# Linear attention beside a gated MLP on one core: a new prologue, tiles turned by DMA, and the up units in one phase

## The chip, the cores and the metric

The kernel runs on one core of one Trainium2 chip. The core has a matrix engine (TensorE, PE in the profile; its weight loads are listed as PEld), a vector engine (VectorE, DVE), an activation engine (ScalarE, ACT), a general engine (GpSimd, POOL) and a queue engine (SyncE, SP), which here only issues transfers. The engines run side by side, each through its own list of instructions in order, and wait for each other on semaphores. Sixteen DMA engines move data. The metric is the device time of one execution in microseconds, smaller is better; shown is the median of the runs.

## The reference

The input x has 2048 tokens of width 512, the attention 32 heads of width 16, the MLP an inner width of 1792. Everything is bfloat16.

```python
xn = _layernorm(x, axis=-1)
return x + _A_ref(xn, A_wqkv, A_w_phi, A_wo) + _B_ref(xn, B_w_gate, B_w_up, B_w_down)

# _A_ref: attention with a softmax feature map
pq = jnp.einsum("bhsd,hdf->bhsf", q, w_phi)
pk = jnp.einsum("bhsd,hdf->bhsf", k, w_phi)
phi_q = jnp.concatenate([_softmax(pq, axis=-1), _softmax(-pq, axis=-1)], axis=-1)
phi_k = jnp.concatenate([_softmax(pk, axis=-1), _softmax(-pk, axis=-1)], axis=-1)
kv = jnp.einsum("bhsf,bhsd->bhfd", phi_k, v)
z  = jnp.einsum("bhsf->bhf", phi_k)
num = jnp.einsum("bhqf,bhfd->bhqd", phi_q, kv)
den = jnp.einsum("bhqf,bhf->bhq", phi_q, z)[..., None] + 1e-6
o = num / den          # then @ wo

# _B_ref: gated MLP without an activation
h = g * u              # g = xn @ w_gate, u = xn @ w_up; then h @ w_down
```

The sums over all tokens in `kv` and `z` split the work into two phases: no query result can be formed before the last key has been added.

## The kernel before

The 2048 tokens are 16 tiles of 128. Every tensor lies in one SBUF arena, and PSUM has eight banks of 512 columns, named by their number.

**Normalization and turning.** `ln_stats` (bn_stats and bn_aggr on DVE, L324 and L325, then Ln and Exp on ACT through the helper at L186) gives mean and inverse deviation, `ln_apply` (DVE, L333) normalizes a tile into one of four `xn` slots, and `x_transpose` turns it: four transposes on PE (L343) into a bank, and a copy by ACT into `xnT`. All matmuls on x read `xnT`.

**Weights.** `w_fold` (L307) multiplies the turned query or key weights by the block-diagonal feature weights, four small matmuls into a bank and a copy by ACT. Folding is done four times for the keys (`w_fold(1, dt)`) and four times for the queries.

**Key and value phase.** For each tile `features("ek", t, 1)` makes the key features: four matmuls of 512 columns (L205, the helper of all the wide matmuls), two exponentials on ACT, a reduce on DVE (L365), a reciprocal (L369) and a ratio (L373), and a product on POOL (L375). `v_stage` makes the values and scales them on DVE (L388; a small copy on POOL at L387). `kv_acc` adds the tile into banks 0 and 1 (L400, eight matmuls of 68 columns). `kv_finish` masks the sums.

**Query phase.** `features("eq", t, 0)` and `q_transpose` (a transposing DMA, L427) make a turned query tile; `num_stage` (L441) multiplies it by the sums into banks 0 and 1, DVE forms the quotient (L449, L452, L453), and another transposing DMA (L457) turns the result. `out_tile` adds 14 matmuls of the MLP's second half and four of the attention's output in one bank; DVE adds x (L490), and the tile is stored (L492).

**Up units.** An `up_unit` is the MLP's first half for 128 inner columns and 512 tokens: eight wide matmuls into a pair of banks, (4, 5) or (6, 7) in turn, a copy of the gate by ACT and a product on DVE (L475). There are 56. The key and value phase has two in each iteration, and the rest stand between the query phase's stages.

**Order.** The steps are recorded in program order, and a planner (`_order`) then forms each engine's list. On PE the program order is kept. On the other engines, and on SP's queue, the planner takes the step that is ready first by its own costs: so many nanoseconds for a step, 200 from one engine to another, and for transfers one stream of 360 bytes a nanosecond in the order of their issue, with 550 for an issue and 1700 for a landing. A step placed on a list waits there on semaphores for what it needs, and everything behind it on that engine waits with it.

Of the kernel before, what the change touches and what calls it, by code (L numbers as in the profile page):

```python
# [16 lines left out]
FF = 1792  # L17
# [4 lines left out]
FSL = 256  # L22
# [4 lines left out]
class _Step:  # L27
    __slots__ = ("eng", "fn", "idx", "deps", "sig", "lane", "semval", "known", "waits", "is_out", "cost", "seq",
                 "finish")

    def __init__(self, eng, fn, idx, lane, cost):
        self.eng = eng
        self.fn = fn
        self.idx = idx
        self.deps = []
        self.sig = False
        self.lane = lane
        self.semval = None
        self.known = {}
        self.waits = []  # L40
        self.is_out = False
        self.cost = cost
        self.seq = 0
        self.finish = 0.0


class _Sched:


    def __init__(self):  # L50
        self.steps = []
        self.writer = {}
        self.readers = {}
        self.dma_count = 0

    def _record(self, st, reads, writes, free=()):
        deps = {}

        def need(d, raw):
            if d is None or d is st:  # L60
                return
            if d.lane == st.lane and (st.eng == PE or not raw):
                return
            deps[id(d)] = d

        for k in reads:
            need(self.writer.get(k), True)
            self.readers.setdefault(k, []).append(st)
        for k in writes:
            w = self.writer.get(k)  # L70
            assert w is None or w is st or self.readers.get(k) or k in reads or st.lane == w.lane or k in free, f"{k} is overwritten unread"
            need(w, False)
            for r in self.readers.get(k, ()):
                need(r, False)
            self.writer[k] = st
            self.readers[k] = []
        st.deps = list(deps.values())

    def step(self, eng, fn, reads, writes, cost):
        st = _Step(eng, fn, len(self.steps), eng, cost)  # L80
        self.steps.append(st)
        self._record(st, reads, writes)
        return st

    def dma(self, eng, fn, reads, writes, nbytes, is_out=False, free=()):
        st = _Step(eng, fn, len(self.steps), ("dma", self.dma_count), nbytes / 360.0)
        self.dma_count += 1
        st.sig = True
        st.is_out = is_out
        self.steps.append(st)  # L90
        self._record(st, reads, writes, free)
        return st
# [18 lines left out]
def _build(nc, es, A_x, A_wqkv, A_w_phi, A_wo, B_w_gate, B_w_up, B_w_down, out):  # L111
# [11 lines left out]
    RK, RQ, RP = 3, 3, 8  # L123
# [17 lines left out]
    alloc("ostg", 3 * 512)  # L141
    alloc("wphi", NQ * 16)
# [8 lines left out]
    alloc("lnv", 2 * NT)  # L151
    alloc("sums", 2 * 16 * 64)
# [60 lines left out]
    mask = sb("mask", 0, CW)  # L213
    eps_f = sbf("eps", 0, 1)
# [28 lines left out]
    def load_gu(eng, s):  # L243
        sl = slice(s * FSL, (s + 1) * FSL)
        load_w(eng, wg_v[:, :, sl], B_w_gate[:, sl].rearrange("(q p) f -> p q f", p=128), ("wg", s), 262144)
        load_w(eng, wu_v[:, :, sl], B_w_up[:, sl].rearrange("(q p) f -> p q f", p=128), ("wu", s), 262144)

    load_w(ACT, wphi_v, bass.AP(tensor=A_w_phi.tensor, offset=A_w_phi.offset, ap=[[16, 128], [2048, NQ], [1, 16]]),
           "wphi", 16384)
    load_x(0, 2)  # L250
    load_qkT(1)
    load_x(2, 2)
    load_w(SP, wv_v, A_wqkv[:, 1024:1536].rearrange("(q p) j -> p q j", p=128), "wv", 524288)
    load_gu(SP, 0)
# [4 lines left out]
    load_qkT(0)  # L259
    load_gu(SP, 3)  # L260
    load_x(12, 4)
    for s in range(4, FF // FSL):
        load_gu(SP, s)
    load_w(SP, wd_v, B_w_down.rearrange("(f p) j -> p f j", p=128), "wd", 1835008)
    load_w(SP, wo_v, A_wo.rearrange("(q p) j -> p q j", p=128), "wo", 524288)


# [33 lines left out]
    def w_fold(w, dt):  # L301
        b = misc_bank()

        def fn(e):
            ins = None
            for jt in range(NQ):
                ins = e.matmul(bank(b, jt * 128, 128), lhsT=wT_v[:, w, jt, dt * 128:(dt + 1) * 128],  # L307
                               rhs=wbd_v[:, jt, :], start=True, stop=True)
            return ins
        sc.step(PE, fn, [("wT", w)] + [("wbd", jt) for jt in range(NQ)], [("ps", b)], 4 * 60.0)  # L310
        act(Wp_v[:, w, dt, :], bank(b), [("ps", b)], [("Wp", w, dt)])
# [5 lines left out]
    rstd = sbf("rstd", 0, NT)  # L317

# [13 lines left out]
    def ln_apply(t):  # L332
        dve(lambda e: e.tensor_scalar(out=xn_tile(t), in0=x_tile(t), scalar1=mv_v[:, t, 0:1], scalar2=rstd[:, t:t + 1],  # L333
                                      op0=ALU.subtract, op1=ALU.mult),
            [("x", t), ("mv", t), ("rstd", t)], [("xn", t % 4)], 512, 0.27)
# [18 lines left out]
    def features(name, t, w):  # L354
        s = t % RK
        e_v = sb(name, s * 1024, 1024).rearrange("p (h k f) -> p h k f", h=H, k=2)
        b = misc_bank() if w else 2
# [24 lines left out]
    def v_stage(t):  # L382
        s = t % RK
        b = misc_bank()
        mm(bank(b), [(xnT(q, t * 128, 128), wv_v[:, q, :]) for q in range(NQ)], [("xnT", t), "wv"], b)
# [49 lines left out]
    def num_stage(t):  # L435
        ph = ph_tile(t)

        def fn(e):
            ins = None
            for c in range(8):  # L440
                ins = e.matmul(bank(c // 4, (c % 4) * CW, CW), lhsT=ph[:, c, :], rhs=kvz_v[:, c, :], start=True,  # L441
                               stop=True)
            return ins
        sc.step(PE, fn, [("phT", t % RP), ("kvz", 0), ("kvz", 1)], [("ps", 0), ("ps", 1)], 8 * 31.0)
        nd = psum[:, 0:1024].rearrange("p (b r) -> p b r", b=2)[:, :, 0:4 * CW].rearrange(
# [5 lines left out]
            [("sums", t % 8), ("ps", 0), ("ps", 1)], [("den", r)], 32)  # L451
# [4 lines left out]
            [("w", r), ("ps", 0), ("ps", 1)], [("o", t % 3)], 512)  # L456
# [6 lines left out]
    def up_unit(ft, sg, pairs):  # L463
# [4 lines left out]
        sl = ft * 128 // FSL  # L468
# [7 lines left out]
            [("ps", bu), ("g", s)], [("hT", ft, sg)], 512)  # L476

    outs = [0]

    def out_tile(t):  # L480
        i = outs[0]
        outs[0] += 1
        b = 3 if ups else 4 + i % 4
        sg = t // 4
        tok = slice(t * 128, (t + 1) * 128)
        mm(bank(b), [(hT_v[:, ft, tok], wd_v[:, ft, :]) for ft in range(NF)],
           [("hT", ft, sg) for ft in range(NF)] + ["wd"], b, stop=False)
        mm(bank(b), [(oT_tile(t)[:, q, :], wo_v[:, q, :]) for q in range(NQ)], [("phT", t % RP), "wo"], b, start=False)
        stg = sb("ostg", (i % 3) * 512, 512)
        dve(lambda e: e.tensor_tensor(out=stg, in0=bank(b), in1=x_tile(t), op=ALU.add),  # L490
            [("ps", b), ("x", t)], [("ostg", i % 3)], 512)
        sc.dma(SP, lambda e: e.dma_start(out_flat[tok, :], stg), [("ostg", i % 3)], [("out", t)], 131072, is_out=True)  # L492
# [3 lines left out]

    def next_up(pairs):
        if ups:
            ft, sg = ups.pop(0)
            up_unit(ft, sg, pairs)  # L500

    PAIRS = [(4, 5), (6, 7)]

    def up(n=1):
        for _ in range(n):
            if ups:
                up_unit(*ups.pop(0), PAIRS)

    ln_stats(0, 1)
    ln_apply(0)  # L510
    ln_stats(1, 1)
    ln_apply(1)
    ln_stats(2, 2)
    for t in range(2, 4):
        ln_apply(t)
    x_transpose(0)
    x_transpose(1)
    for dt in range(NQ):
        w_fold(1, dt)
    x_transpose(2)  # L520
    x_transpose(3)
    wq_steps = [lambda dt=dt: w_fold(0, dt) for dt in range(NQ)]
    for t in range(NT + 2):
        if t < NT:
            features("ek", t, 1)
        if t in (0, 2, 4):
            ln_stats(4 + 2 * t, 4)
        up()
        if 2 * t + 4 < NT:
            ln_apply(2 * t + 4)  # L530
            x_transpose(2 * t + 4)
        elif wq_steps and t >= 6:
            wq_steps.pop(0)()
        if 0 <= t - 1 < NT:
            v_stage(t - 1)
        up()
        if 2 * t + 5 < NT:
            ln_apply(2 * t + 5)
            x_transpose(2 * t + 5)
        elif wq_steps and t >= 6:  # L540
            wq_steps.pop(0)()
        if t >= 2:
            kv_acc(t - 2)
        if t >= NT - 1:
            features("eq", t - NT + 1, 0)
            q_transpose(t - NT + 1)
            up()
    kv_finish()
    up()
    oq = list(range(NT))  # L550
    for t in range(NT):
        if t + 3 < NT:
            features("eq", t + 3, 0)
            q_transpose(t + 3)
        up()
        num_stage(t)
        up()
        if t >= 2:
            out_tile(oq.pop(0))
    up(len(ups))  # L560
    while oq:
        out_tile(oq.pop(0))
# [10 lines left out]
def _order(sc):  # L573
# [9 lines left out]
    fixed = {PE: [st for st in steps if st.eng == PE]}  # L583
# [9 lines left out]
    while len(order) < len(steps):  # L593
        best = None
        for e, lst in ready.items():
            if e in fixed:
                lst = [p for p in lst if p[1] == fixed[e][pos[e]].idx] if pos[e] < len(fixed[e]) else []
# [9 lines left out]
        if e in fixed:  # L607
            pos[e] += 1
        st = steps[idx]
        if isinstance(st.lane, tuple):  # L610
# [98 lines left out]
```

## Time and profile before

| | us |
|---|---|
| median of three runs | 237.48 |
| lowest and highest | 235.88, 238.23 |
| the profiled execution | 238.51 |
| its span, first to last instruction | 236.8 |

| engine | busy us | share of the span |
|---|---|---|
| PE | 218.5 | 92% |
| PEld | 105.5 | 45% |
| DVE | 146.0 | 62% |
| ACT | 82.7 | 35% |
| POOL | 42.8 | 18% |

In the lines of the profile a row names the source line, the engine, the operation, what is written and read with its shape, a count, and then the busy time and the mean duration of one in nanoseconds, and the idle time before it with what ended it. A timeline or chain row begins with its start and its length in microseconds. "Releaser" is what an idle engine was waiting for last. A slice string has 40 digits, one for each fortieth of the span (5.92 us), in tenths. A windows row has the stretch and its length, the busy time and count of PE, PEld, DVE, ACT and POOL (or of PE alone), and then the clock granted to PE, with 1.00 for full, the mean busy share of the DMA engines and the GB/s moved.

### The profile page before, as it was taken

How to read it: one execution, taken by the hardware profiler on the slowest of the kernel's cores; microseconds unless marked ns; L12 is line 12 of the kernel's file. 1: busy time of each engine (PE TensorE's matmuls, PEld its weight loads, DVE VectorE, ACT ScalarE, POOL GpSimd, SP SyncE). 2: the span in 40 equal slices, each digit the busy share in tenths (PEclk: the TensorE clock that was granted, in tenths of full speed). 3: DMA queues.
4: the chain of work that ended last, by engine and by line, in shares of the span. 5: the costliest groups of instructions: out<-in, count | busy, mean ns of one | idle time of the engine just before them, and what ended most of it. 6: DMA issues, size and time to landing. Idle time of an engine off the chain costs nothing.

```text
span 236.8 us, 3283 instructions
## 1 busy us (share of the span) xinstructions
PE 218.5 (92%) x1255; PEld 105.5 (45%) x1280; DVE 146.0 (62%) x282; ACT 82.7 (35%) x157; POOL 42.8 (18%) x65
## 2 busy tenths in 40 slices
PE   0397969999999999999999999999999999999994
PEld 0243424555544444444444444444444454444441
DVE  2369995766666666666657784654564567775421
ACT  3374626555543343334344541232132132110000
POOL 6002220222222223321211211101101111111000
PEclk9999988999999999999999999999999999999999
DMA  7999990000000000000022265064125135754411
GB/s 150 324 261 281 312 312 6 1 3 0 0 3 0 0 0 3 0 0 3 0 46 44 44 93 106 27 91 89 22 66 91 32 82 116 125 114 89 69 46 44
DMA packets 44993, 18.32 MB, mean 77 GB/s; under 512 B 30897, under 2 KB 44977, under 8 KB 44977
## 3 DMA queue, kind: packets, MB, share of 16 engines
q1 hardware_dynamic: 44448, 18.09, 33.6%
q8 instruction: 10, 0.16, 0.3%
q10 hardware_dynamic: 528, 0.02, 0.1%
q14 instruction: 7, 0.05, 0.1%
HBM read 8.67 MB, written 2.10 MB: 45 GB/s over the span
## 4 chain that ended last, share of the span: by engine, by line
PE 89%; DVE 3%; DMA 2%; issue 2%; ACT 1%; SPq 1%
PE ps L205 83%; PE ps L343 2%; DMA arena<-in_A_x_dram 2%; PE ps L441 2%; PE ps L400 2%; ACT arena L186 1%; SPq L241 1%; PE ps L307 1%; DVE arena L475 1%; DVE arena L324 1%; DVE arena L365 0%; DVE arena L369 0%; DVE arena L333 0%; DVE arena L490 0%; SPq L226 0%
## 5 line engine op out<-in xcount | busy, mean ns | idle before, releaser
L205 PE MATMUL ps<-arena 128*128 128x512 bf16 x903 | 207.7, 383 | 1.4
L205 PEld LDWEIGHTS ps<-arena 128*128 128x128 bf16 x928 | 88.5, 98 | 101.9 <-issue 3.3
L186 ACT ACTIVATE arena<-ps 128x512 bf16<-128x512 f32 (+1 forms) x144 | 79.6, 597 | 124.0 <-PE ps L205 108.2
L365 DVE TENSOR_REDUCE arena<-arena 128x64 f32<-128x1024 bf16 x32 | 38.9, 1216 | 33.9 <-ACT arena L186 33.9
L375 POOL TENSOR_TENSOR arena<-arena 128x512 bf16<-128x512 bf16 x32 | 34.0, 1061 | 90.6 <-DVE arena L373 86.1
L475 DVE TENSOR_TENSOR arena<-ps,arena 128x512 bf16<-128x512 f32 x56 | 38.4, 685 | 12.8 <-PE ps L205 12.8
L490 DVE TENSOR_TENSOR arena<-ps,arena 128x512 bf16<-128x512 f32 x16 | 11.1, 691 | 30.0 <-PE ps L205 30.0
L387 POOL CAST arena<-arena 128x32 bf16<-128x32 f32 x16 | 5.2, 326 | 78.5 <-DVE arena L369 75.0
L343 PE MATMUL ps<-arena 128*128 128x128 bf16 x64 | 6.9, 242 | 13.4 <-DVE arena L333 13.1
L324 DVE BATCH_NORM_STATS2 arena<-arena 128x6 f32<-128x512 bf16 x16 | 10.3, 672 | 6.9 <-DMA arena<-in_A_x_dram 6.9
L343 PEld LDWEIGHTS ps<-arena 128*128 128x128 bf16 x64 | 5.1, 108 | 17.4 <-DVE arena L333 14.1
L453 DVE TENSOR_TENSOR arena<-ps,arena 128x512 bf16<-128x512 f32 x16 | 11.1, 691 | 0.5
L388 DVE TENSOR_TENSOR arena<-ps,arena 128x512 bf16<-128x512 f32 x16 | 10.2, 636 | 0.1
L369 DVE RECIPROCAL arena<-arena 128x64 f32<-128x64 f32 x16 | 8.7, 542 | 0.0
L333 DVE TENSOR_SCALAR arena<-arena 128x512 bf16<-128x512 bf16 x16 | 7.1, 486 | 1.6 <-ACT arena L186 1.6
L441 PEld LDWEIGHTS ps<-arena 128*128 128x128 bf16 x128 | 6.2, 97 | 3.8
L400 PEld LDWEIGHTS ps<-arena 128*128 128x128 bf16 x128 | 5.9, 97 | 2.4
L441 PE MATMUL ps<-arena 128*128 128x68 bf16 x128 | 6.7, 194 | 0.0
L400 PE MATMUL ps<-arena 128*128 128x68 bf16 x128 | 6.7, 194 | 0.0
L373 DVE TENSOR_TENSOR arena<-arena 128x32 f32<-128x32 f32 x32 | 5.9, 184 | 0.2
L452 DVE RECIPROCAL arena<-arena 128x32 f32<-128x32 f32 x16 | 5.6, 349 | 0.3
L371 DVE RECIPROCAL arena<-arena 128x32 f32<-128x32 f32 x16 | 5.5, 347 | 0.2
(17 smaller groups left out, 20.1 us busy)
## 6 DMA issues: line engine op xcount, KB each, us to landing
out_dram<-arena SPq DMA_DIRECT2D x16, 128.0 KB, 1.7
arena<-in_B_w_gate_dram SPq DMA_DIRECT2D x7, 256.0 KB, 6.0
arena<-in_B_w_up_dram SPq DMA_DIRECT2D x7, 256.0 KB, 6.0
arena<-in_B_w_down_dram SPq DMA_DIRECT2D x1, 1792.0 KB, 10.1
arena<-in_A_x_dram SPq DMA_DIRECT2D x3, 512.0 KB, 6.3
arena<-in_A_x_dram SPq DMA_DIRECT2D x2, 256.0 KB, 3.6
arena<-in_A_wqkv_dram SPq DMA_DIRECT2D x1, 512.0 KB, 5.0
arena<-in_A_wo_dram SPq DMA_DIRECT2D x1, 512.0 KB, 10.7
```

Source lines behind the costliest of these rows:

```text
L186: return sc.step(ACT, lambda e: e.activation(out=out_ap, in_=in_ap, func=func, scale=scale, **kw), reads, writes, 130.0 + 0.833 * n)
L205: ins = e.matmul(out_ap, lhsT=l, rhs=r, start=start and i == 0, stop=stop and i == npair - 1, **kw)
L324: dve(lambda e, t=t: e.bn_stats(stats_v[:, t, 0:6], x_tile(t)), [("x", t)], [("st", t)], 512)
L343: ins = e.transpose(bank16(b, q * 128, 128), xn_tile(t)[:, q * 128:(q + 1) * 128], ident)
L365: dve(lambda e: e.tensor_reduce(out=sm, in_=e_v, axis=AX.X, op=ALU.add), [(name, s, 0), (name, s, 1)], [("sums", sr)], 1024)
L375: pool(lambda e: e.tensor_tensor(out=e_v[:, :, 1, :], in0=e_v[:, :, 1, :], in1=rat[:, :, None].to_broadcast([128, H, 16]), op=ALU.mult), [ ...
L388: dve(lambda e: e.tensor_tensor(out=vs_tile(t)[:, :, 0:16], in0=bank(b).rearrange("p (h f) -> p h f", h=H), in1=rp.unsqueeze(2).to_broadca ...
L400: ins = e.matmul(bank(c // 4, (c % 4) * CW, CW), lhsT=ek[:, c * 128:(c + 1) * 128], rhs=vs[:, c * CW:(c + 1) * CW], start=(t == 0 and c % ...
L441: ins = e.matmul(bank(c // 4, (c % 4) * CW, CW), lhsT=ph[:, c, :], rhs=kvz_v[:, c, :], start=True, stop=True)
L453: dve(lambda e: e.tensor_tensor(out=o_tile(t).rearrange("p (b h f) -> p b h f", b=2, f=16), in0=nd[:, :, :, 0:16], in1=w_v[:, r].unsqueeze ...
L475: dve(lambda e: e.tensor_tensor(out=hT_v[:, ft, sg * 512:(sg + 1) * 512], in0=bank(bu), in1=g, op=ALU.mult), [("ps", bu), ("g", s)], [("hT ...
L490: dve(lambda e: e.tensor_tensor(out=stg, in0=bank(b), in1=x_tile(t), op=ALU.add), [("ps", b), ("x", t)], [("ostg", i % 3)], 512)
```

## The change

**Loads.** x comes as tile 0, tile 1, tiles 2 and 3, and then in fours. The value weights, the feature weights and the first gate and up slice are issued on ACT's queue. The slices of gate and up are now one of 256 columns and three of 512. The last slice, tiles 12 to 15, the turned query weights and the two output weights are issued on SP within iterations 1, 3 and 5 of the key and value phase.

**Pinning.** Steps recorded while `sc.pin` is set keep their order among themselves on every engine, as all PE steps do; the others may still be placed between them.

**Prologue.** DVE zeroes 512 columns (in the place of `hT`), and PE multiplies them 16 times into bank 5. Then come statistics of tiles 0 and 1, their normalization, statistics of tiles 2 and 3, the transposes of tiles 0 and 1, normalization of tiles 2 and 3, the values of tiles 0 and 1 in banks 0 and 1 (scaled later), the transposes of tiles 2 and 3, and the key folds, whose evictions alternate between ACT and DVE. One up unit follows.

**Tiles 4 to 15** are normalized by ACT (a scale and a bias, the bias by POOL) and turned by a DMA from SP instead of PE and ACT.

**Phases.** The key and value phase has three up units in most iterations; in its last iterations `features` and `q_transpose` of query tiles 0 to 5 are added. The query phase has no up units but one at its start: for each tile a `num_stage`, the `out_tile` of the tile before, and the features of the tile seven ahead. `num_stage` alternates between banks 0, 1 and 2, 3. The last output tile is made in two halves of 256 columns. The key features have four slots instead of three.

```diff
-FSL = 256
+SLICES = [(0, 256), (256, 512), (768, 512), (1280, 512)]
...
+    sc.pin = True
+    load_x(0, 1)
+    load_w(ACT, wv_v, A_wqkv[:, 1024:1536].rearrange("(q p) j -> p q j", p=128), "wv", 524288)
+    load_x(1, 1)
+    load_x(2, 2)
     load_w(ACT, wphi_v, ...
-    load_x(0, 2)
     load_qkT(1)
-    load_x(2, 2)
-    load_w(SP, wv_v, ...
-    load_gu(SP, 0)
+    load_gu(ACT, 0)
     load_x(4, 4)
     load_gu(SP, 1)
     load_gu(SP, 2)
     load_x(8, 4)
+    sc.pin = False
...
+    dve(lambda e: e.memset(zero, 0.0), [], ["zero"], 256)
...
     def ln_apply(t):
+        if t < 4:
+            dve(...)
+            return
+        nb = nbias[:, t:t + 1]
+        pool(lambda e: e.tensor_scalar(out=nb, in0=mv_v[:, t, 0:1], scalar1=rstd[:, t:t + 1], scalar2=-1.0,
+                                       op0=ALU.mult, op1=ALU.mult), [("mv", t), ("rstd", t)], [("nb", t)], 1)
+        act(xn_tile(t), x_tile(t), [("x", t), ("rstd", t), ("nb", t)], [("xn", t % 4)], func=ACTF.Identity,
+            scale=rstd[:, t:t + 1], bias=nb)
+
+    def x_turn(t):
+        o = sb("xnT", 0, NQ * S_TOK).rearrange("p (q s) -> p q s", q=NQ)[:, :, t * 128:(t + 1) * 128]
+        sc.dma(SP, lambda e: e.dma_start_transpose(o, xn_tile(t)), [("xn", t % 4)], [("xnT", t)], 131072)
...
+    sc.pin = True
+    warm(16)
     ln_stats(0, 1)
+    ln_stats(1, 1)
     ln_apply(0)
-    ln_stats(1, 1)
     ln_apply(1)
-    ln_stats(2, 2)
-    for t in range(2, 4):
-        ln_apply(t)
+    ln_stats(2, 1)
+    ln_stats(3, 1)
     x_transpose(0)
     x_transpose(1)
-    for dt in range(NQ):
-        w_fold(1, dt)
+    ln_apply(2)
+    ln_apply(3)
+    v_matmul(0, 0)
+    v_matmul(1, 1)
     x_transpose(2)
     x_transpose(3)
+    for dt in range(NQ):
+        w_fold(1, dt, (2, 3, 6, 7)[dt])
+    sc.pin = False
+    up()
...
     for t in range(NT + 2):
         if t < NT:
             features("ek", t, 1)
-        if t in (0, 2, 4):
-            ln_stats(4 + 2 * t, 4)
+        if t % 2 == 0 and 4 + t < NT:
+            ln_stats(4 + t, 2)
         up()
...
+        x_next(t + 4)
+        late_loads(t)
+        if 2 <= t - 1 < NT:
+            b = misc_bank()
+            v_matmul(t - 1, b)
+            v_scale(t - 1, b)
+        if t < 2:
+            v_scale(t, t)
+        else:
+            up()
             kv_acc(t - 2)
+            up()
+        if 7 < t < 12:
+            w_fold(0, t - 8)
+        if t >= NT - 4:
+            features("eq", t - NT + 4, 0)
+            q_transpose(t - NT + 4)
+        if t >= NT - 2:
             up()
     kv_finish()
...
+    q_next(6)
+    up(len(ups))
+    num_stage(0)
+    q_next(7)
+    for t in range(1, NT):
         num_stage(t)
+        out_tile(t - 1)
+        q_next(t + 7)
+    out_tile(NT - 1, 2)
...
-    fixed = {PE: [st for st in steps if st.eng == PE]}
+    fixed = {e: [st.idx for st in steps if st.eng == e and st.pin] for e in (PE, ACT, DVE, POOL, SP)}
...
-                lst = [p for p in lst if p[1] == fixed[e][pos[e]].idx] if pos[e] < len(fixed[e]) else []
+            if pos[e] < len(fixed[e]):
+                lst = [p for p in lst if not steps[p[1]].pin or p[1] == fixed[e][pos[e]]]
```

## What is predicted

> **What bounds the kernel now.** I read the busy shares and slices first, then the chain, then PE's timeline.
>
> ```profile
> span 236.8 us, 3283 instructions
> PE   0397969999999999999999999999999999999994
> GB/s 150 324 261 281 312 312 6 1 3 0 0 3 0 0 0 3 0 0 3 0 46 44 44 93 106 27 91 89 22 66 91 32 82 116 125 114 89 69 46 44
> PE 89%; DVE 3%; DMA 2%; issue 2%; ACT 1%; SPq 1%
> L205 PEld LDWEIGHTS ps<-arena 128*128 128x128 bf16 x928 | 88.5, 98 | 101.9 <-issue 3.3
> ...
> 14.51 1.90 PE ps L205 x4
> ...
> 22.24 0.22 PE ps L343 x4
> 22.46 2.59 PE ps L205 x12
> ...
> 131.38 0.26 PE ps L441 x8
> ...
> 233.91 0.69 DVE arena L490
> ```
>
> PE carries 89% of the chain, and its slices are full from the seventh to the last: there only less PE work helps. The chain gives full-speed prices: a wide matmul 2.59/12 = 0.216 us, a tile's four transposes 0.22, a fold (four matmuls of the same shape) as much, and eight small matmuls of `kv_acc` or `num_stage` 0.26. There are 928 wide matmuls (by their weight loads; some matmul records are missing), 16 transposed tiles, 8 folds and 32 groups of small ones: 200.3 + 3.5 + 1.8 + 8.2 = 213.8 us. The last matmul ends at 233.9, so PE loses 20.1 us, and 2.9 us follow it.
>
> ```profile
> 9.19 1.04 PE L343 MATMUL ps<-arena 128*128 128x128 bf16 x8 [9.19 <-DVE arena L333]
> 14.51 3.99 PE L205 MATMUL ps<-arena 128*128 128x512 bf16 x12
> 20.12 0.40 PE L343 MATMUL ps<-arena 128*128 128x128 bf16 x4 [1.62 <-DVE arena L333]
> ...
> 32.98 0.40 PE L343 MATMUL ps<-arena 128*128 128x128 bf16 x4 [2.30 <-DVE arena L333]
> 33.22 4.44 PE L205 MATMUL ps<-arena 128*128 128x512 bf16 x12
> ...
> 3.86 1.29 DVE L324 BATCH_NORM_STATS2 arena<-arena 128x6 f32<-128x512 bf16 x2 [3.86 <-DMA arena<-in_A_x_dram]
> 8.12 0.70 DVE L324 BATCH_NORM_STATS2 arena<-arena 128x6 f32<-128x512 bf16 x1 [2.76 <-DMA arena<-in_A_x_dram]
> 8.73 0.72 DVE L333 TENSOR_SCALAR arena<-arena 128x512 bf16<-128x512 bf16 x2
> ...
> 12.94 1.29 DVE L324 BATCH_NORM_STATS2 arena<-arena 128x6 f32<-128x512 bf16 x2 [0.29 <-DMA arena<-in_A_x_dram]
> ...
> 15.46 0.30 DVE L325 BATCH_NORM_AGGREGATE arena<-arena 128x2 f32<-128x6 f32 x2
> ```
>
> All 20 us are lost before 37.5: 9.2 before the first transposes, 3.6 in the thin prologue (1.76 us of work in 5.32), 1.4 on slow matmuls from 14.51, gaps of 1.6 and 2.3, and 1.7 on the slow dozen from 33.2. The DVE rows give the cause: DVE runs in order, and the planner had put the statistics of tile 2 ahead of tile 0's normalization. They waited for x until 8.12, so tile 0 was normalized only at 8.73, though its own statistics had begun at 3.86. The later gaps end on the same kind of wait.
>
> **The change, part by part.** PE's work first. Twelve tiles leave PE for the transposing DMA: 12 x 0.22 = 2.6 us less. The split of the last output keeps its columns, and eight matmuls of 68 columns in 0.26 us show that weight loads hide well below 256 columns: 0. That leaves 211.2 us. The dummies run before any tile is ready. Should all 16 run as slowly as the four that took 1.90 from 14.51, 0.475 each, they fill 7.6 us from about 1.3 and end at 8.9; at the full rate they end at 4.8. The first copies on ACT begin at 8.45 in any case (next), so at worst 0.5 to 1 us, and that is hidden by a later wait of 2.3: 0.
>
> ```profile
> L186 ACT ACTIVATE arena<-ps 128x512 bf16<-128x512 f32 x128 | 70.2, 597 | 110.1 <-PE ps L205 108.2 <-PE ps L307 1.7
> 5.26 0.71 ACT L186 ACTIVATE arena<-arena 128x1 f32<-128x1 f32 x4 [3.17 <-DVE arena L325]
> 0.81 0.44 SPq L226 DMA_DIRECT2D arena<-in_A_x_dram  x1
> 1.31 2.60 SPq L241 DMA_TRANSPOSE arena<-in_A_wqkv_dram  x1
> 3.97 0.56 SPq L226 DMA_DIRECT2D arena<-in_A_x_dram  x1
> ```
>
> Prologue. Tiles 2 and 3 are now issued at 1.8 instead of 3.97, ahead of the 2.6 us issue of the key weights, but beside value weights on ACT's queue. Bounds for their landing: 4.9 (3.05 us after issue, as tiles 0 and 1) and 8.1 (as now); I take 6.0, because 0.5 MB of x and 0.5 MB of values, at some 250 GB/s between the first two slices (150 and 324), need 4 us after the first 2. Their two statistics end at 7.9, and ACT, whose pinned order puts the copies of tiles 0 and 1 behind their Ln and Exp, copies at 8.45 to 9.65 (0.6 each). Then `v_matmul` 0 and 1 (1.7) to 10.8, transposes 2 and 3 to 11.3, their copies to 12.4. The first fold uses the bank of tile 3's transpose, so folds run 12.5 to 13.4, and the first up unit (8 x 0.216) to 15.1. By then PE has done 16 wide matmuls, four tiles and four folds: 3.45 + 0.88 + 0.88 = 5.2 us. So 206.0 us remain from `features(0)` on, which could begin at 15.1.
>
> It will not, I think. Pinned steps keep their order only among themselves; loose ones may slip between, by the planner's modelled landing. It models tiles 4 to 7 as landed just after `ln_apply(3)` and the folds much later, so all four statistics of 4 to 7 stand on DVE ahead of the two fold evictions now given to DVE, and their Ln and Exp on ACT ahead of the other two. Now these tiles land at 12.94. The same 2.6 MB stand ahead of them, in two queues; I take 12.5 (bounds 11.3, where the slices' sum reaches 2.6 MB, and 12.94). Four statistics took 2.8 us (12.94 to 15.76): 15.3. Ln and Exp 0.9: 16.2. Two evictions on ACT 1.2: `features(0)` at 17.4, a PE gap of 2.3 us.
>
> The Trainium skill, DMA: Bandwidth & Descriptors, section Issuing engines are not separate DMA queues, says that issuing from several engines saves only the sequencer's issue time, since the same 16 DMA engines carry all. By it the tiles would land at 12.94 as before and the sum below would be 0.4 us longer. The row agrees so far as it shows a 2.6 us issue in front of x.
>
> ```profile
> 12.90:17.50 4.60, 4.29 (x19) 1.80 (x18) 2.82 (x8) 3.01 (x7) 0.00 (x0) 1.00 1.25 266
> 17.50:33.00 15.50, 11.48 (x64) 5.40 (x65) 15.42 (x33) 7.96 (x18) 3.13 (x5) 1.00 1.07 303
> ...
> L365 DVE TENSOR_REDUCE arena<-arena 128x64 f32<-128x1024 bf16 x32 | 38.9, 1216 | 33.9 <-ACT arena L186 33.9
> L475 DVE TENSOR_TENSOR arena<-ps,arena 128x512 bf16<-128x512 f32 x56 | 38.4, 685 | 12.8 <-PE ps L205 12.8
> L369 DVE RECIPROCAL arena<-arena 128x64 f32<-128x64 f32 x16 | 8.7, 542 | 0.0
> L388 DVE TENSOR_TENSOR arena<-ps,arena 128x512 bf16<-128x512 f32 x16 | 10.2, 636 | 0.1
> L373 DVE TENSOR_TENSOR arena<-arena 128x32 f32<-128x32 f32 x32 | 5.9, 184 | 0.2
> L375 POOL TENSOR_TENSOR arena<-arena 128x512 bf16<-128x512 bf16 x32 | 34.0, 1061 | 90.6 <-DVE arena L373 86.1
> ```
>
> A second block of this kind follows. Between tiles 4 to 7 and 8 to 11 stand wider slices, 2.1 MB, and 0.5 MB of x itself: 2.62 MB at 303 GB/s is 8.6 us, a landing at about 21.1. The planner lets three of their statistics (2.2 with an aggregate) go ahead of `features(0)`'s sums: reduce ends at 24.3, the product of the second up unit at 25.0. Its banks are wanted by the fourth unit, which PE reaches at 17.4 + 3 x 0.86 + 2 x 1.73 = 23.4: 1.6 us. The next product waits for recip, reduce, ratio, value scaling (0.54 + 1.22 + 0.18 + 0.64) and ends 3.2 after: 1.5 more; the third wait is 0.1. Together 3.2 us. Bounds: 0 and 4.6 (landing as in the rivals).
>
> After that an iteration has 32 wide matmuls, 7.2 us, against 1.22 + 0.54 + 0.18 + 0.64 + 3 x 0.69 + 0.84 = 5.5 on DVE and about 3.9 on ACT, where tile 4 on are now normalized: 0. POOL's small bias step precedes that on ACT; bounded by POOL's row, 0 to 1.06 a tile, hidden by four iterations of lead. On SP each turn waits for ACT, and behind it wait the last gate slice, tiles 12 to 15, query weights and both output weights. The earliest needed, the gate slice, is used only in iteration 4, about 14 us after its turn in the queue: 0.
>
> ```profile
> L457 SPq DMA_TRANSPOSE arena<-arena x16: 1189/1196/1271, 135.2 to 223.9; - x16
> DMA to landing us min/median/max: 2.4/2.4/4.2
> ...
> SPq L457 <- DVE arena L453: 34.1, 10, 5.3
> ...
> 222.61 0.18 DVE L449 SCALAR_TENSOR_TENSOR arena<-arena,ps 128x32 f32<-128x32 f32 x1
> ...
> 223.21 0.69 DVE L453 TENSOR_TENSOR arena<-ps,arena 128x512 bf16<-128x512 f32 x1
> ```
>
> The query phase loses its up units, its cover. A tile there is 22 wide matmuls and a `num_stage`, 5.0 us. From `num_stage(t)` to its turned result: 1.3 on DVE (222.61 to 223.90) and 2.4 landing, 3.7. PE needs it behind `out_tile(t-1)`, features, `num_stage(t+1)` and 14 matmuls: 3.9 + 0.9 + 0.3 + 3.0 = 8.0. Cover holds. Only the first tile has no `out_tile` before it: 4.4 after the start of its `num_stage`, against 0.26 + 3.7 + one reduce 1.22 = 5.2: 0.8 us once (0 to 2). At the end only half of the tile is evicted last, half of 0.69: 2.9 becomes 2.6.
>
> Sum: 17.4 + 206.0 + 3.2 + 0.8 + 2.6 = 230.0 us of span. The profiled execution took 238.51 with a span of 236.8, 1.71 outside, and the median 237.48 lies 1.03 below it. So 231.7 on its terms, 230.7 for the median.
>
> **The rivals.**
> Through: tiles 4 to 11 block nobody; `features(0)` starts at 15.1: 15.1 + 206.0 + 0.8 + 2.6 = 224.5, median 225.2. For it: the prologue's own order is pinned. Against: the rows at 8.12 and 12.94 show DVE held by x.
> Half: tiles 4 to 7 block, 8 to 11 land in time: 226.8 of span. Here the clock counts.
>
> ```profile
> 34.00:34.50 0.50, 0.50 (x4) 0.60 1.02 320
> ...
> 37.50:38.00 0.50, 0.50 (x14) 0.99 0.00 0
> ```
>
> After the idle 2.30 us, granted clock fell to 0.5 from 34.2 to 37.5: half of 3.4 us, 1.7, is lost. My gap of 2.3 would do likewise: 228.5, median 229.2. In the forecast itself this loss lies under DVE's debt. TensorE: Matmul & The Clock Gate, Part 1 of the Trainium skill, gives an idle window of about 3.4 us before the clock halves; by it this rival would give 226.8. The row disagrees: 2.30 sufficed.
> Debt: tiles 4 to 7 land at 12.94, and 2.62 MB go at 266 GB/s, so 8 to 11 land at 22.8. That is 0.4 more for the start, 1.4 more of debt, and 1.7 if the clock's loss adds: 233.5, median 234.2. The change then nearly fails at its purpose.
> Slower: SP holds each turned result behind the next query turn. That one is ready 3.9 + 0.9 + 1.2 + 1.2 + 0.5 + 1.06 = 8.7 after `num_stage(t)`; with 1.25 issue and 2.4 landing, the result comes at 12.4 instead of 8.0, and eight tiles lose 4.4: 35 us, median 266. It decides from 0.85 a tile (6.8 over eight). Against: SP's waits at L457 are for that tile's own DVE result, so it stands in front.
>
> **How the numbers follow.** Forecast 0.41, half 0.17, through 0.24, debt 0.13, slower 0.05. I predict 230.7. From 224.0 to 235.0: the low end cuts the part of "through" in which tiles 2 and 3 land at 4.9 and the first output waits for nothing (223.3), the high end the rest of "debt" and "slower". A measurement tells about 1% from no change, so faster means below 235.1: three cases and 0.05 of "debt", 0.87; the rest of "debt", 0.08, is the same; slower 0.05.
>
> **What would show it.** First transposes near 6 to 8, `v_matmul` 0 near 9; `features(0)` near 17 behind ACT or DVE, with DVE's idle there ended by x; DVE without idle around 21 to 30; a saturated PE after; waits under 1 us at the first output. PE's end before 220 would refute the two blocks, PE gaps at every query tile the cover.

## The result and the profile after

| | before | changed |
|---|---|---|
| median us | 237.46 | 230.31 |
| lowest and highest | 235.88, 238.23 | 229.74, 231.65 |
| profiled execution, span | 238.51, 236.8 | 229.74, 228.0 |

The ratio is 0.9715, with a 95% interval from 0.9649 to 0.9782: the changed kernel is faster, by 7.15 us of the medians. The forecast was 230.7. The two profiled spans differ by 8.8 us, and the account below is made between them. One execution of a later run, the one without dummies, fell into a slow state (238.79 us, the five others 230.63 to 232.16) and is left out of its median below.

First the page of the changed kernel: its span, PE's slices, and the shares of the chain that ended last.

```profile
span 228.0 us, 3302 instructions
PE   7389999999999999999999999989999999999995
PE 92%; DVE 2%; DMA 2%; ACT 2%; issue 1%; SPq 0%; DVEq 0%
```

The slices are full from the fourth on instead of the seventh. The digit 7 at the start is no gain: those are the dummy matmuls. PE's timeline of the changed kernel shows the front row by row (start, length, what, and in brackets the idle time before it).

```profile
1.26 4.97 PE L536 MATMUL ps<-arena 128*128 128x512 bf16 x16 [1.26 <-DVE arena L273]
7.02 0.40 PE L365 MATMUL ps<-arena 128*128 128x128 bf16 x4 [0.79 <-DVE arena L345]
7.83 0.40 PE L365 MATMUL ps<-arena 128*128 128x128 bf16 x4 [0.42 <-DVE arena L345]
10.49 3.29 PE L212 MATMUL ps<-arena 128*128 128x512 bf16 x8 [2.26 <-ACT arena L193]
13.58 0.94 PE L365 MATMUL ps<-arena 128*128 128x128 bf16 x8
15.47 1.05 PE L314 MATMUL ps<-arena 128*128 128x128 bf16 x16 [0.96 <-ACT arena L193]
16.37 11.39 PE L212 MATMUL ps<-arena 128*128 128x512 bf16 x52
...
151.50 1.04 PE L212 MATMUL ps<-arena 128*128 128x512 bf16 x4 [1.05 <-DVE arena L500]
```

The chain of the same kernel puts the end of the folds at 16.53, and its later rows give the steady price.

```profile
1.25 4.36 DMA arena<-in_A_x_dram
...
15.47 1.05 PE ps L314 x16
16.53 11.22 PE ps L212 x52
27.75 0.26 PE ps L423 x8
28.01 6.91 PE ps L212 x32
...
157.54 0.26 PE ps L466 x8
157.79 4.75 PE ps L212 x22
...
225.51 0.42 DVE arena L517
```

Here the whole change can be read. From 16.53 to the end PE waits once, 1.05 us at 151.50. Up to 16.53 it has done 3.5 us of useful work (eight wide matmuls, four tiles, four folds at full rate), so 13.0 are lost in front, against 20.1 before. That is 7.1 of the 8.8 us. The turned tiles give 2.6 (12 x 0.22), the shorter end 0.4 (228.0 less 225.5 against 2.9), and the new wait takes 1.05. These make 9.05; small pauses take the rest. No run takes the new front back alone, or parts its loads from its pinned order, so the 7.1 us rest on the waits in the two profiles.

Three things in these rows matter later. The eight value matmuls took 3.29 us where eight take 1.73 at full rate. They waited 2.26 us for ACT. And no gap at all stands before the first features, which follow the first up unit at 18.3. The clock explains the first. These are half-microsecond windows of PE in the changed kernel (length, busy time and count of PE, granted clock, DMA share, GB/s).

```profile
2.00:2.50 0.50, 0.50 (x2) 1.00 0.82 207
...
10.50:11.00 0.50, 0.50 (x2) 0.84 1.08 336
11.00:11.50 0.50, 0.50 (x3) 0.50 1.11 352
...
13.50:14.00 0.50, 0.50 (x5) 0.50 1.05 334
14.00:14.50 0.50, 0.50 (x6) 0.75 1.14 361
```

The dummies had done what they are there for. 16 in 4.97 us is 0.31 each, between the full rate of 0.216 and half of it: they began slowly, two in the window at 2.00 against four in a window at full rate, although the granted clock reads 1.00 there. Then PE did nothing for 2.26 us, and soon after the real work began the granted clock fell to 0.50 for some 3.4 us. So PE is slow in two ways here: at a granted clock of 0.50, and in its first work, where the profile's clock shows nothing.

DVE's timeline of the changed kernel answers to the rows shown of before.

```profile
5.64 0.69 DVE L335 BATCH_NORM_STATS2 arena<-arena 128x6 f32<-128x512 bf16 x1 [1.57 <-DMA arena<-in_A_x_dram]
...
6.46 0.50 DVE L345 TENSOR_SCALAR arena<-arena 128x512 bf16<-128x512 bf16 x1
...
11.63 1.29 DVE L335 BATCH_NORM_STATS2 arena<-arena 128x6 f32<-128x512 bf16 x2 [1.16 <-DMA arena<-in_A_x_dram]
...
16.12 1.29 DVE L321 CAST arena<-ps 128x512 bf16<-128x512 f32 x2 [1.67 <-PE ps L314]
...
19.17 1.29 DVE L335 BATCH_NORM_STATS2 arena<-arena 128x6 f32<-128x512 bf16 x2 [0.18 <-DMA arena<-in_A_x_dram]
...
20.45 0.66 DVE L335 BATCH_NORM_STATS2 arena<-arena 128x6 f32<-128x512 bf16 x1
21.03 1.20 DVE L387 TENSOR_REDUCE arena<-arena 128x64 f32<-128x1024 bf16 x1
22.15 0.68 DVE L500 TENSOR_TENSOR arena<-ps,arena 128x512 bf16<-128x512 f32 x1
```

Tile 0 is normalized (L345) at 6.46 instead of 8.73. The order is the forecast one: the statistics of tiles 4 to 7 before the fold evictions (L321), and three of tiles 8 to 11 before the first reduce (L387). But here DVE waits 1.67 us for the folds themselves, so its statistics held up no eviction. What differs is how late that was: x landed at 11.6 and 19.2 instead of 12.5 and 21.1.

### The profile page after: what moved, and what is told of

Its sections match the earlier page's. It is cut to its first block, busy times and chain, and to the rows that moved or that the text cites. A ratio compares the mean times of both kernels' runs of the same rounds, so it can differ in the third digit from the quotient of the medians.

```text
span 228.0 us, 3302 instructions
## 1 busy us (share of the span) xinstructions
PE 218.7 (96%) x1266; PEld 105.7 (46%) x1266; DVE 146.9 (64%) x276; ACT 83.3 (37%) x161; POOL 45.3 (20%) x77
## 4 chain that ended last, share of the span: by engine, by line
PE 92%; DVE 2%; DMA 2%; ACT 2%; issue 1%; SPq 0%; DVEq 0%
PE ps L212 88%; DMA arena<-in_A_x_dram 2%; PE ps L423 2%; PE ps L466 2%; ACT arena L193 2%; PE ps L314 1%; DVE arena L335 1%; DVE arena L500 0%; DVE arena L336 0%; DVE arena L345 0%; DVE arena L387 0%; PE ps L365 0%; DVE arena L517 0%; SPq L234 0%; DVEq L724 0%
## 5 line engine op out<-in xcount | busy, mean ns | idle before, releaser
L212 PE MATMUL ps<-arena 128*128 128x512 bf16 (+1 forms) x946 | 208.0, 377 | 3.3 <-ACT arena L193 2.3
L212 PEld LDWEIGHTS ps<-arena 128*128 128x128 bf16 x946 | 90.3, 98 | 103.5 <-ACT arena L193 2.4
L193 ACT ACTIVATE arena<-ps 128x512 bf16<-128x512 f32 (+1 forms) x128 | 70.0, 597 | 100.0 <-PE ps L212 95.6
L387 DVE TENSOR_REDUCE arena<-arena 128x64 f32<-128x1024 bf16 x32 | 38.7, 1214 | 20.7 <-ACT arena L193 20.7
L500 DVE TENSOR_TENSOR arena<-ps,arena 128x512 bf16<-128x512 f32 x56 | 38.3, 685 | 21.3 <-PE ps L212 20.8
L517 DVE TENSOR_TENSOR arena<-ps,arena 128x512 bf16<-128x512 f32 (+1 forms) x17 | 11.2, 660 | 23.7 <-PE ps L212 23.7
L193 ACT ACTIVATE arena<-arena 128x2 f32<-128x2 f32 (+2 forms) x32 | 13.8, 460 | 9.6 <-DVE arena L336 5.8
L478 DVE TENSOR_TENSOR arena<-ps,arena 128x512 bf16<-128x512 f32 x16 | 11.1, 691 | 0.5
L411 DVE TENSOR_TENSOR arena<-ps,arena 128x512 bf16<-128x512 f32 x16 | 10.4, 649 | 0.1
L423 PEld LDWEIGHTS ps<-arena 128*128 128x128 bf16 x128 | 6.2, 97 | 3.8
L466 PEld LDWEIGHTS ps<-arena 128*128 128x128 bf16 x128 | 6.2, 97 | 3.8
L395 DVE TENSOR_TENSOR arena<-arena 128x32 f32<-128x32 f32 x32 | 6.8, 213 | 0.4
L536 PE MATMUL ps<-arena 128*128 128x512 bf16 x16 | 5.0, 480 | 1.3 <-DVE arena L273 1.3
L350 POOL TENSOR_SCALAR arena<-arena 128x1 f32<-128x1 f32 x12 | 2.9, 265 | 15.1 <-ACT arena L193 15.1
```

Of the source, the lines that this page charges most:

```text
L193: return sc.step(ACT, lambda e: e.activation(out=out_ap, in_=in_ap, func=func, scale=scale, **kw), reads, writes, 130.0 + 0.833 * n)
L212: ins = e.matmul(out_ap, lhsT=l, rhs=r, start=start and i == 0, stop=stop and i == npair - 1, **kw)
L387: dve(lambda e: e.tensor_reduce(out=sm, in_=e_v, axis=AX.X, op=ALU.add), [(name, s, 0), (name, s, 1)], [("sums", sr)], 1024)
L411: dve(lambda e: e.tensor_tensor(out=vs_tile(t)[:, :, 0:16], in0=bank(b).rearrange("p (h f) -> p h f", h=H), in1=rp.unsqueeze(2).to_broadca ...
L423: ins = e.matmul(bank(c // 4, (c % 4) * CW, CW), lhsT=ek[:, c * 128:(c + 1) * 128], rhs=vs[:, c * CW:(c + 1) * CW], start=(t == 0 and c % ...
L466: ins = e.matmul(bank(b0 + c // 4, (c % 4) * CW, CW), lhsT=ph[:, c, :], rhs=kvz_v[:, c, :], start=True, stop=True)
```

## The experiments

The theory after the profile: PE is the bound from 16.5 on, and the front is a chain through the landing of tile 1, DVE's statistics in pinned order, ACT's copies behind them, and the values at half clock. Behind that chain stand the two blocks that the prediction named, just covered. The rivals: the dummies do save something; or the blocks are not there; or the gain came from moving the up units.

All ratios are to the kernel before on the same chip. The first four runs stand beside each other, then the next four, then the last four.

| run | median us | ratio | 95% interval |
|---|---|---|---|
| changed kernel again | 231.67 | 0.9787 | 0.9752 to 0.9822 |
| no dummies | 230.71 | 0.9764 | 0.9729 to 0.9798 |
| dummies up to the first value | 231.98 | 0.9802 | 0.9774 to 0.9831 |
| turned on PE | 232.53 | 0.9847 | 0.9809 to 0.9885 |
| copies first | 227.53 | 0.9595 | 0.9563 to 0.9628 |
| copies first, statistics later | 226.75 | 0.9563 | 0.9528 to 0.9597 |
| up units in both phases | 233.37 | 0.9838 | 0.9788 to 0.9888 |
| bank 5 | 234.19 | 0.9889 | 0.9851 to 0.9928 |
| more dummies, statistics later | 228.83 | 0.9655 | 0.9626 to 0.9683 |
| output weights later | 230.82 | 0.9745 | 0.9712 to 0.9779 |
| best front, new change of phase | 225.45 | 0.9512 | 0.9487 to 0.9538 |
| the same, output weights later | 225.53 | 0.9513 | 0.9487 to 0.9538 |

**The changed kernel again.**

> The changed kernel once more, as the mark for the runs beside it: 230.3 us, span 228 to 230, first wide matmuls near 10.5 at half clock, PE saturated from about 15.5.

The median is 231.67, 1.4 above the first one, and the ratio 0.9787. Span 230.0. PE's timeline of this run has a wait that the first profile did not have:

```profile
10.97 2.90 PE L212 MATMUL ps<-arena 128*128 128x512 bf16 x8 [2.27 <-ACT arena L193]
...
50.86 1.04 PE L212 MATMUL ps<-arena 128*128 128x512 bf16 x4 [0.93 <-ACT arena L193]
52.22 6.22 PE L212 MATMUL ps<-arena 128*128 128x512 bf16 x27 [0.33 <-DVE arena L500]
```

ACT's and SP's timelines of the same run say what ACT was doing then:

```profile
48.53 0.81 ACT L193 ACTIVATE arena<-arena 128x512 bf16<-128x512 bf16 x1 [4.27 <-DMA arena<-arena]
...
36.89 0.58 SPq L245 DMA_DIRECT2D arena<-in_B_w_down_dram  x1
37.51 0.93 SPq L245 DMA_DIRECT2D arena<-in_A_wo_dram  x1
38.81 13.91 SPq L357 DMA_TRANSPOSE arena<-arena  x6
```

A normalization needs an `xn` slot whose tile is being turned, and that turn is issued behind 2.36 MB of output weights. ACT works through its list in order, so the up units' gate copies wait behind it.

**No dummies.**

```diff
-    warm(16)
```

> The 16 dummy matmuls are left out, nothing else. Theory (the dummies end 4 us before the first wide matmul, so the clock is slow there with or without them): no difference, 230.3 within 1 us. Rival (the dummies save the slow start that the kernel before paid from 14.5 on): 1.7 us slower, 232.

230.71 against 231.67, with overlapping intervals of the ratios: no difference that can be told.

```profile
11.09 3.59 PE L212 MATMUL ps<-arena 128*128 128x512 bf16 x8 [2.05 <-ACT arena L193]
```

The eight value matmuls take 3.59 us in this profile, 3.29 and 2.90 in the two with the dummies. The reason is another one: the granted clock reads 1.00 from 11.0 to 14.6 here, and 0.50 in most of that stretch with the dummies. Without dummies the values are PE's first wide matmuls and run slowly like the first dummies. The first up unit starts at 17.4 instead of 16.7, and the waits behind it are shorter (0.28 us in all before the change of phase, 1.43 in the run beside it). So, as placed, the dummies are worth nothing measurable in the total; what they save in front, up to 0.8 us, the later waits cover in these two profiles.

**Dummies up to the first value.**

```diff
+    warm(9)
     v_matmul(0, 0)
     v_matmul(1, 1)
```

> Nine more dummies between the transposes of tiles 0 and 1 and the first value matmul, to fill the 2.26 us gap. Theory (half clock from 10.6 to 14.2 lies on the path that sets the start): the eight value matmuls take 1.7 instead of 3.3 us, the first up unit starts near 14.7 instead of 16.5, 228.5 us. Rival (the statistics of tiles 4 to 7 hold the first features in any case, as predicted): a new gap before the first features, which start at 17.4 or later, and at most 0.9 us less.

A miss for the theory: 231.98, no gain. Its timeline shows why.

```profile
10.63 1.90 PE L212 MATMUL ps<-arena 128*128 128x512 bf16 x8 [0.32 <-ACT arena L193]
...
15.13 1.67 PE L212 MATMUL ps<-arena 128*128 128x512 bf16 x7
17.16 8.81 PE L212 MATMUL ps<-arena 128*128 128x512 bf16 x40 [0.36 <-ACT arena L193]
27.24 1.04 PE L212 MATMUL ps<-arena 128*128 128x512 bf16 x3 [1.27 <-DVE arena L500]
...
29.66 6.22 PE L212 MATMUL ps<-arena 128*128 128x512 bf16 x28 [0.27 <-DVE arena L500]
```

The values run at full rate, and the first up unit starts 1.5 us earlier than in the run beside it. PE then meets what the prediction named: the first features behind ACT, at 17.2, and up units behind DVE's products. What the clock gives, 1.5 us, the two blocks take: the waits of 0.36, 1.27 and 0.27 us, where the run beside it has 0.17 before 30.

**The same with the statistics later.**

```diff
+            sc.pin = True
             ln_stats(4 + t, 2)
+            sc.pin = False
```

> The nine more dummies of before, and the statistics of tiles 4 on pinned behind the fold evictions. Theory (with the clock kept full, what the longer dummies gained was given back to exactly the two waits of the prediction, first features behind the statistics of tiles 4 to 7 and up units behind those of 8 to 11): the gaps of 0.3, 0.4, 1.3 and 0.3 us between 15 and 30 go, first features near 16.9, 1.5 to 2 us less than with the longer dummies alone. Rival (DVE has too much work there in any order): the gaps stay.

228.83, or 0.0147 less in the ratio, 3.5 us: more than the expected 1.5 to 2. In its timeline one wait is left between 15 and 150:

```profile
26.66 0.41 PE L423 MATMUL ps<-arena 128*128 128x68 bf16 x8 [0.28 <-DVE arena L411]
```

The surplus has a reason: in this order ACT's wait for the output weights is gone as well (4.05 us with the longer dummies alone, where PE lost 0.71 and 0.33 behind it; none listed here). So both blocks are shown, and DVE has not too much work there, only the wrong order.

**Copies first, without and with the statistics later.**

```diff
+    x_transpose(0)
+    x_transpose(1)
     ln_stats(2, 1)
     ln_stats(3, 1)
-    x_transpose(0)
-    x_transpose(1)
```

> Transposes of tiles 0 and 1 are recorded before the statistics of tiles 2 and 3, so that ACT copies them before those tiles' Ln and Exp. Theory: first value matmul near 8.1 instead of 10.5, at full clock, folds near 11.4 to 12.5, first up unit from about 12.4; then the statistics of tiles 4 to 7 (their Ln and Exp stand on ACT ahead of the fold evictions) set the first features near 16.5 instead of 18.3, and the gap of about 2.5 us may halve the clock once: 228.5 us, 230.2 with the clock. Rival (the start is bound by landing of weights): no difference.

227.53, a little better than either figure. The block of tiles 4 to 7 stands open in its PE timeline:

```profile
8.30 1.90 PE L212 MATMUL ps<-arena 128*128 128x512 bf16 x8
...
15.94 9.66 PE L212 MATMUL ps<-arena 128*128 128x512 bf16 x43 [1.26 <-DVE arena L336]
```

DVE's timeline of the same run shows what stands in front:

```profile
13.95 0.67 DVE L335 BATCH_NORM_STATS2 arena<-arena 128x6 f32<-128x512 bf16 x1
14.52 1.27 DVE L321 CAST arena<-ps 128x512 bf16<-128x512 f32 x2
```

The values start at 8.30 and at full clock, 2.2 us earlier, and PE then waits 1.26 us before the first features. The row names L336, a statistic, but the features read no statistic: they need the folded weights, whose evictions on DVE (L321) end at 15.8, behind three statistics of tiles 4 to 7.

> The same, and the statistics of tiles 4 on are pinned too, so that none stands ahead of the fold evictions. Theory: first features near 14.2, PE without a gap from about 11.5: 4 us less than the changed kernel, 226.3. If instead tiles 8 to 11 then hold DVE (the debt of the prediction): gaps of up to 3 us between 18 and 28.

226.75 against the expected 226.3. In its timeline the first up unit and the features follow without a gap, and DVE's debt does not appear:

```profile
13.24 11.17 PE L212 MATMUL ps<-arena 128*128 128x512 bf16 x50
24.70 0.41 PE L423 MATMUL ps<-arena 128*128 128x68 bf16 x8 [0.28 <-DVE arena L411]
```

**Turning on PE.**

```diff
-            x_turn(t)
+            x_transpose(t)
```

> Tiles 4 to 15 are turned by PE and copied by ACT again, normalization stays on ACT. Theory (PE is saturated from 16.5 on, so its work counts in full): 12 x 0.22 = 2.6 us slower, 233.0. Rival (the turning DMA was itself late, or PE has slack there): 0 to 1 us.

232.53, 0.9 us slower than the run beside it, or 1.4 by the ratios, with wide intervals: about half of what was expected. PE does 2.6 us more, but its timeline has no wait between 16.8 and the change of phase, where the run beside it waits 0.17, 0.93 and 0.33: 1.4 us come back. The turning DMA saves PE work and, behind the output weights, brings a wait of its own.

**Output weights later.**

```diff
-        elif t == 5:
+        elif t == 12:
             load_w(SP, wd_v, ...
```

> The changed kernel with both output weights loaded in iteration 12 instead of 5, behind the last turned tile on SP. Theory (ACT's normalization waits 4.3 us near 44 to 48 for a slot whose turn stands in the DMA queue behind 2.3 MB of weights, and PE loses 0 to 1.3 us to it): ACT's wait there goes, and 0 to 1.3 us of time. Rival (the turns are slow in themselves): ACT's wait stays.

ACT's wait is gone, so it is the weights in front of the turn. The time is 230.82, within the spread of the changed kernel. This profile happens to keep its clock over the same 2.26 us gap:

```profile
10.79 1.90 PE L212 MATMUL ps<-arena 128*128 128x512 bf16 x8 [2.26 <-ACT arena L193]
...
17.11 8.81 PE L212 MATMUL ps<-arena 128*128 128x512 bf16 x40 [0.15 <-ACT arena L193]
27.21 1.04 PE L212 MATMUL ps<-arena 128*128 128x512 bf16 x4 [1.28 <-DVE arena L500]
29.63 6.22 PE L212 MATMUL ps<-arena 128*128 128x512 bf16 x28 [0.27 <-DVE arena L500]
```

It is the forecast case in kind: features at 17.1 behind ACT, then waits on DVE's products, 1.6 us instead of 3.2.

**Up units in both phases.** Two up units in an iteration, the others in pairs in the query phase, with the banks of the kernel before.

> The key and value phase has two up units in an iteration, the rest stand in the query phase, two a tile, with the banks of the kernel before; prologue, loads and turning DMA stay as changed. Theory (PE is saturated in both layouts, so the place of the up units is worth nothing but the wait of 1 us at the change of phase): 229.3 to 230.3. Rival (moving the up units is what gained): back by 3 us or more, 233.

The time is what the rival named, 233.37, but the reason is another. The layout brings a wait of its own, because `num_stage` has only banks 0 and 1 again:

```profile
127.27 0.63 PE L466 MATMUL ps<-arena 128*128 128x68 bf16 x8 [3.03 <-DVE arena L478]
```

That is 2.0 us more than the changed kernel's 1.05 at the change of phase. The granted clock reads 0.50 from about 126.9 to 130.2, which costs some 1.4 us more (half of the 2.9 us of work in that stretch). The wait of 3.03 is PE's only one after the prologue in this run, so elsewhere the place of the up units costs PE nothing. The six executions go with the clock: 231.81 and 232.04 where its mean was 1.0, and 233.05 to 234.75 where it was 0.985 or 0.978. By the ratios this layout is 0.0051 or 1.2 us slower than the changed kernel measured again, and 0.0123 or 2.9 us slower than its first measurement. The wait and the clock behind it account for either. So these runs show no gain from the move itself, but the two kernels were not measured side by side.

**Bank 5.**

```diff
-            features("eq", t, 0, 3 if t == 6 else 6 + t % 2)
+            features("eq", t, 0, 3 if t == 6 else 5 if t == 7 else 6 + t % 2)
```

> The features of query tile 7 go into bank 5 instead of 7, which the last up unit still holds. Theory: the 1.05 us wait at 150.5 goes, 229.3. Rival (the first output then waits for its turned result, as predicted, 0.8): no difference or 0.2.

A miss, and slower: 234.19. The wait for the bank is gone, and the wait for the turned result, which the prediction had put at 0.8 us, takes its place at 3.0:

```profile
153.50 4.34 SPq L450 DMA_TRANSPOSE arena<-arena  x2
...
157.89 2.57 SPq L482 DMA_TRANSPOSE arena<-arena  x2
...
160.50 2.00 PE L212 MATMUL ps<-arena 128*128 128x512 bf16 x6 [3.01 <-DMA arena<-arena]
```

The planner reordered DVE's and SP's lists with the bank: the first result's turn is issued at 157.89 here, behind one query turn more, and at 152.95 in the changed kernel. The clock pays a second time: it reads 0.50 from about 161.3 to 164.7, worth 1.7 us. The wait, 2.0 longer than before, and the clock make 3.7; the ratio lies 0.0102 to 0.0174 above the changed kernel's two, 2.4 to 4.1 us.

**The best front with a new change of phase.**

```diff
     q_next(6)
-    up(len(ups))
     num_stage(0)
+    up(len(ups))
     q_next(7)
```

> Copies first and statistics later (the fastest so far, 226.8), and at the change of phase the last up unit behind the first num_stage, the features of query tile 7 behind it in bank 5. Theory: features of tile 7 no longer wait for the bank, and the last up unit covers part of the turn of the first result: the 1.05 us at the change goes or is halved, 225.7 to 226.3. Rival (as with bank 5 alone, the wait for the turned result takes its place in full): 226.8 to 228.8.

> The same with the output weights in iteration 12. Theory: as the one before or up to 0.5 us less, 225.2 to 226.3.

With copies first, statistics later and bank 5, 225.45, a little better than the theory; with the output weights later too, 225.53, the same. No PE wait above 0.3 us is listed after the folds, at the change of phase neither. Both beat the changed kernel and the kernel before (0.9512 and 0.9513).

## Why the prediction was right, and where its terms were not

**Work: right.** An iteration takes 6.91 + 0.26 = 7.17 us (7.2 forecast), a query tile 5.01 (5.0), and the end 2.5 (2.6). In the sum of PE's work before, 32 groups of 0.26 us are 8.3 and not 8.2, which changes nothing.

**First values at 9.1: wrong by 1.4.** They began at 10.49. I let tiles 2 and 3 set the chain, landing at 6.0. Tile 1 set it: issued alone beside the value weights, it landed 4.36 us after its issue, at 5.61, and the pinned order puts its normalization ahead of the statistics of tiles 2 and 3.

**Dummies at 0: right as a delay, wrong as a gain.** They ended at 6.2, before the first transposes, and delayed nothing. But the sum also priced the eight value matmuls behind them at the full rate, 1.7 us, and they took 3.29 at a granted clock of 0.50. The dummies end so early that the clock can be lost again, and this I had looked for only later in the front.

**First features at 17.4, block of tiles 4 to 7: the mechanism is shown, in the first profile not binding.** With the values late and slow, PE reached the features only at 18.3, and DVE had finished. As soon as PE is earlier, the block appears: at 17.16 with the longer dummies and 17.11 with the output weights later, and at 15.94 with copies first. The gap in front was forecast at 2.3 us; it was 0.36, 0.15 and 1.26, because the values came later than forecast in the first two.

**Debt of 3.2: right mechanism, too large.** It was 0 in the first profile and about 1.6 in the two that kept their clock with the statistics where I had them (longer dummies; output weights later). Two steps were mis-sized. The landing of tiles 8 to 11 was set at 21.1 by the old rate of 303 GB/s, while the rows at 10.5 to 14.5 show 334 to 361; it was 19.2 in the first profile and 20.3 in those two. And I let a whole up unit wait for DVE's product. Only its second bank does; the gate's bank is freed by ACT's copy. So the four gate matmuls, 0.86 us, still run in front of the wait: 40 wide matmuls stand from the first features to the wait of 1.27 us, where three features and three units make 36. A slow clock does lie under the two blocks, as the longer dummies showed, though it fell on the values and not behind the gap where the sum had it.

**Change of phase at 0.8: near in size, wrong cause.** The 1.05 us are a bank, held by the last up unit. The turned result I named cost 3.0 once the bank did not, in the order that the planner then made.

**Turns on SP at 0: wrong.** I looked at what waits behind the turns, not at what the turns wait behind. ACT stood 1.7 to 4.3 us for a slot in six of the profiles that kept the loads' order, and PE lost up to 1.3 of it; in the first profile ACT stood 2.73 and PE lost nothing.

**Rivals.** The condition of "through" (224.5), that tiles 4 to 11 block nobody, held in the first profile; its time did not come, because the features began at 18.3 and not at 15.1. The last two runs, with spans of 223.7 and 223.8, have both an early start and no block. "Half" and "debt" differ from the forecast only in what covers what, and neither fits the first profile. Of "slower" nothing was seen in the changed kernel: in the query phase the turned result stands in front on SP, and cover holds. With bank 5 the first result stood behind the turn of query tile 7, once. The Trainium skill's idle window of about 3.4 us (TensorE: Matmul & The Clock Gate, Part 1) disagrees with the runs: 2.26 us were enough in the first profile, though not in every one. By the Trainium skill's sentence on issuing engines (DMA: Bandwidth & Descriptors, Issuing engines are not separate DMA queues) tiles 4 to 7 would have landed at 12.94; they landed at 11.6 in the first profile and at 12.75 in the run with the longer dummies, so it is not far off.

The total came out as close as 0.4 us by luck in part. Against the forecast span of 230.0, the first profile has 0.9 more in front, 3.2 less of debt, 0.25 more at the change of phase, 0.1 less at the end and 0.2 of small pauses: 228.0. And from a profiled span to the median the sum added 0.7 us, as before; this time it was 2.3, because the profiled execution was the fastest of its four, where the one before was slower than its three. The case that the sum describes, features near 17.1 behind ACT and then a debt, is seen whole only in the two later profiles, with spans of 230.3 and 228.8.

## What to carry to other kernels

When a planner fills in-order queues by modelled landing times, look in each queue for a step that waits on a transfer and stands ahead of a step that the critical engine needs: moving it back gained 3.5 us here, where keeping the clock full had gained nothing by itself. A wait that the critical engine does not show may only be covered by an earlier one; take the earlier one away and read again before counting its gain. Dummy work that ends well before the real work may have lost its effect by then. What the full clock is worth once the two blocks are gone was not measured by itself.

## What was not expected of the hardware

The same idle gap of PE, 2.26 us after the same 16 dummies, halved the granted clock in the first profile (0.50 from 11.0 to 14.0) and left it full in another, the one with the output weights later, where the eight matmuls behind it took 1.90 instead of 3.29 us. Five of the six profiles with this gap lost the clock. Whether such a gap costs anything therefore differs from one execution to the next, and a single profile does not settle it. Of the ten executions of the changed kernel, two have a mean granted clock of 1.0; they took 229.97 and 231.65 us, inside the range of the eight others, 229.74 to 233.06.

The granted clock of the profile does not show every slow matmul. Without dummies it reads 1.00 while the first eight wide matmuls take 3.59 us, 0.45 each.
